# Score matmuls of two attention units, in 64-row halves of the matrix array

## The chip, the cores and the metric

The kernel runs on one core of one Trainium2 chip. A core has a matrix engine (TensorE, PE in the profile, whose weight loads are listed as PEld), a vector engine (VectorE, DVE), a scalar engine (ScalarE, ACT), a general engine (GpSimd, POOL) and a sync engine that issues DMAs (SP); they run their own instruction streams in order and wait for each other through semaphores. Matmuls read the on-chip memory SBUF (128 partitions) and write PSUM, whose banks hold 128 x 512 fp32 values each. The metric is the device time of one execution in microseconds (us).

## The reference

One transformer block over 2048 positions of width 576. The part that the change touches is an attention with 32 heads of 18 features, in 4 segments of 512 positions, with a memory carried from one segment to the next:

```python
for s in range(N):                                   # 4 segments
    qs, ks, vs = q[:, :, s], k[:, :, s], v[:, :, s]
    logits = einsum("bhqd,bhkd->bhqk", qs, ks) * scale + mask      # mask: causal, within the segment
    p = softmax(logits); a_dot = einsum("bhqk,bhkd->bhqd", p, vs)
    num = einsum("bhld,bhde->bhle", phi(qs), M); den = einsum("bhld,bhd->bhl", phi(qs), z) + 1e-6
    outs.append(g * num / den + (1 - g) * a_dot)                   # g = sigmoid(beta) per head
    M = M + einsum("bhld,bhle->bhde", phi(ks), vs); z = z + sum_l phi(ks)
x = x + ga * (concat(outs) @ wo)
x = x + gb * ((silu(h @ w_gate) * (h @ w_up)) @ w_down)            # h: normalised x, F = 4608
```

Everything is fp32. The kernel reaches that accuracy with products of split numbers: a value is a high part, rounded to the matrix engine's fp32r form, plus a low part, and a product is high*high + low*high + high*low.

## The kernel before, in words

The program has three stages, one after the other on the matrix engine.

**Projections (0 to about 234 us of the span).** For each segment the normalised input is multiplied by wq, wk and wv (`proj`, `vproj`). The results go to DRAM buffers: `kD[s]` holds, for each feature, the high part twice and the low part once, `qD[s]` high, low, high. Three rows per feature times 18 features are 54 rows, so that one matmul over 54 rows forms the three split products of a head's score at once. In this stage `early()` (L262) also runs the first pass of units 0 and 1, between the projections, in an order that a scheduler picks.

**The unit loop (about 234 to 582 us).** A unit is 4 heads of one segment; there are 32 (8 per segment). The order here is written out by hand (`tc.manual_schedule`). Each unit has two passes over its causal scores.

- Pass 1 (`p1_step`, L175, matmuls on L189) finds the row maxima: for each of four blocks of 128 queries (i = 3 to 0) and each head it makes scores against n = 128 (i + 1) keys in a PSUM bank (tag `s1`, 2 buffers, with a spare bank for early units), and DVE adds the causal mask `tri` and takes the maximum (L194, one reduction a head). POOL splits the negated maxima into a high and a low part (L199 to L202), PE transposes them (`mt_a`, L208), ACT copies them out, and `put_m` (L170) sends them by DMA as two additional rows of the unit's query stack.
- Pass 2 (`p2_step`, L609, matmuls on L624) makes the transposed scores for each of four blocks of 128 keys (j = 0 to 3) against n = 512 - 128 j queries. The two additional rows meet rows of ones on the key side, so that the maxima are subtracted in the same matmul. ACT takes exp (L627) from the PSUM bank (tag `s2`, 2 buffers) to `Pt`, and POOL clears the part above the diagonal. `av_step` (L635, matmuls on L644) then multiplies by the values: four heads go to four strips of 32 output columns.

A unit's stack (`new_stack`, L121, `load_stack`, L161; 4 sets of buffers) has 108 rows for keys, two heads of 54 rows above each other, in two column blocks, plus two rows of ones. On the query side each of the four heads has its own column block of 108 rows, of which the 54 rows of the other head of the pair are zero (cleared once by ACT, L125), so that a matmul over 108 rows gives one head's scores. With two heads side by side in the query stack, pass 2 covers two heads of n = 256 or 128 with one matmul.

The loop (L1367) walks u = 0 to 32, with pass 2 of unit u and pass 1 of unit u + 2 in the same 11 steps. At each step it takes one piece of either pass (one bank of scores and its evacuation), then the events of `PAT` (L61, four patterns by unit): V0 to V3 are the value matmuls, m and n the transposed maxima, c and d the combination with the memory part, A, B, C, D, G the memory reads of the next segment, M, X, R, S, T, Z the output projection of the segment before (`wo_m`, matmuls on L753), Q, q, P, Y the preparation of wo. Feed-forward preparations for the next stage are hung onto fixed steps.

**Feed-forward (about 582 us to the end).** The two up-projections (matmuls on L1209) and the down-projection (L1318, L1337) fill the rest.

Of the kernel before, what the change touches and what calls it, by code (L numbers as in the profile page):

```python
# [15 lines left out]
P = 128  # L16
S = 2048
D = 576
# [4 lines left out]
L = 512  # L23
# [33 lines left out]
NE = 2  # L57
WQ = (0, 3, 4, 5, 6)
E1 = 3
E2 = 2  # L60
PAT = (["", "M0", "V2 V3 m E D", "n", "M1 Q G", "c", "M2 d", "V0", "h A0 q M3 R S X", "T Y Z B0", "A1 P V1 z B1 f C"],  # L61
# [3 lines left out]
LNA = 1  # L65
S1B, S2B, XB, WB = 2, 2, 2, 1


def f32(ap):
    return ap.bitcast(F32)  # L70
# [3 lines left out]
def block(ctx: ExitStack, tc: tile.TileContext, x, wqk, wv, wo, beta, wgu, wd, c, w_mod, wm01, out):  # L74
    nc = tc.nc
# [7 lines left out]
    def chain(*g):  # L83
        for a in g:
            yield from a
# [20 lines left out]
    ident = cst.tile([P, P], F32, tag="ident", name="ident")  # L106
# [3 lines left out]
    ones = cst.tile([P, P], F32, tag="ones", name="ones")  # L110
# [5 lines left out]
    NB = 4  # L116
    sk = pool(mid, "sk")
    mwk = pool(mid, "mwk", 2)
    qst, kst = {}, {}

    def new_stack(b, stk):  # L121
        qst[b] = stk.tile([P, 4, L], F32R, tag=f"qs{b}", name=f"qs{b}")
        kst[b] = stk.tile([P, 2, L], F32R, tag=f"ks{b}", name=f"ks{b}")
        for a in range(0, 4, 2):
            nc.scalar.mul(qst[b][:, a:a + 2].rearrange("p a (b c) -> p (a b) c", c=P),  # L125
                          ones.unsqueeze(1).to_broadcast([P, 8, P]), 0.0)
        nc.sync.dma_start(f32(kst[b][108:110]).rearrange("p a (b c) -> p (a b) c", c=P),
                          ones[0:2, :].unsqueeze(1).to_broadcast([2, 8, P]))

    tri = vst.tile([P, L], F32, tag="tri", name="tri")  # L130
    nc.gpsimd.memset(tri, 0.0)
# [23 lines left out]

    units = [(s, q) for s in range(NSEG) for q in range(8)]
    NU = len(units)
    mcol, pmt, mrow = {}, {}, {}
    turn = [0, 0]

    def load_stack(u, b):  # L161
        s, q = units[u]
        for e in range(2):
            v = [d[s].rearrange("f z t -> (f z) t").rearrange("(Q a e r) t -> Q e r a t", Q=8, a=2, e=2)[q, e]
                 for d in (kD, qD)]
            r = slice(54 * e, 54 * e + 54)
            nc.sync.dma_start(f32(kst[b][r]), v[0])
            nc.sync.dma_start(f32(qst[b][r, e:4:2, :]), v[1])

    def put_m(u, b):  # L170
        mr = mrow.pop(u)
        for a in range(2):
            nc.sync.dma_start(f32(qst[b][108 + a:109 + a]).rearrange("p a t -> p (a t)"), mr[16 * a:16 * a + 16])

    def p1_step(u, b, i, ps, jp, jb, spare=0):  # L175
        if i == 3:
            mcol[u] = (mwk.tile([P, 4, 4], F32, tag="mx", name="mx"),
                       mwk.tile([P, 2, 4, 4], F32R, tag="mc", name="mc"))
        mx, mc = mcol[u]
        n = 128 * (i + 1)  # L180
        per = L // n if n <= 256 else 1
        for h0 in range(0, 4, per):
# [5 lines left out]
            for h in range(h0, h0 + per):  # L188
                nc.tensor.matmul(bank[:, n * (h - h0):n * (h - h0) + n],  # L189
                                 lhsT=qst[b][0:108, h, 128 * i:128 * i + 128],  # L190
                                 rhs=kst[b][0:108, h // 2, 0:n], start=True, stop=True)
            for h in range(h0, h0 + per):
                junk = jp.tile([P, L], BF16, tag="junk", name="junk", bufs=jb)
                nc.vector.tensor_tensor_reduce(junk[:, :n], bank[:, n * (h - h0):n * (h - h0) + n], tri[:, L - n:],  # L194
                                               1.0, -3e38, op0=ALU.add, op1=ALU.max, accum_out=mx[:, h, i:i + 1])
            if h0 + per < 4:
                yield
        if i == 0:
            nc.gpsimd.tensor_scalar(mc[:, 0], mx, -1.0, 0.0, op0=ALU.mult, op1=ALU.add)  # L199
            lo = mwk.tile([P, 4, 4], F32, tag="ml", name="ml")  # L200
            nc.gpsimd.tensor_tensor(lo, mx, f32(mc[:, 0]), op=ALU.add)
            nc.gpsimd.tensor_scalar(mc[:, 1], lo, -1.0, 0.0, op0=ALU.mult, op1=ALU.add)  # L202
        yield

    def mt_a(u, ps, tag, bufs):
        mc = mcol.pop(u)[1]
        pmt[u] = ps.tile([P, L], F32, tag=tag, name="pmt", bufs=bufs)
        nc.tensor.transpose(pmt[u][:32, :P], f32(mc).rearrange("p a b c -> p (a b c)"), ident)  # L208

    def mt_b(u):  # L210
        mrow[u] = mr = mwk.tile([32, P], F32, tag="mr", name="mr")
# [41 lines left out]
    with ExitStack() as p1:  # L253
# [5 lines left out]
        wk = pool(p1, "wk1", 2)  # L259
        ps = pool(p1, "ps1", 2, space=PSUM)  # L260

        def early():  # L262
            for u in range(2):
                load_stack(u, u)
            for u in range(NE):
                yield from p1_unit(u, u, ps, "m", 1, pb, 2)
            load_stack(2, 2)

# [65 lines left out]
        with ExitStack() as p0:  # L334
# [12 lines left out]
            for i in range(4):  # L347
                mv, rs = ln_stats(wk, [xs[0][:, i, :]], 1)
# [7 lines left out]
            for k in (4, 0, 1, 2, 3):  # L356
                for p in (1, 0):
                    for h in range(2):
                        r = 64 * (1 - p) + 32 * h
                        a = slice(0, P) if k < 4 else slice(64 - 64 * p, 128 - 64 * p)  # L360
                        w = wm[:, 1 + 2 * k + p] if k < 4 else wm[a, 0]
                        last = nc.tensor.matmul(pr[r:r + 32, :320], lhsT=sgb[a, k, :], rhs=w[:, 256 * h:256 * h + 320],
                                                start=(k == 4), stop=(k == 3))
# [10 lines left out]
            for b in range(3):  # L374
                n = P if b < 2 else 64
# [7 lines left out]
        pb = pool(p1, "pb", 2)  # L383
# [151 lines left out]
        for s in range(NSEG):  # L535
# [5 lines left out]
            g = chain(*gens)  # L541
# [6 lines left out]
            for t in QKORD:  # L548
# [4 lines left out]
                f = proj(s, t)  # L553
# [45 lines left out]
        if u < NU:  # L599
            load_stack(u, u % NB)  # L600

    def p1_seq(u):
        if NE <= u < NU:
            for i in range(4):
                yield from p1_step(u, u % NB, 3 - i, ps, wk, 4, WB if u < 11 else 0)

    Pt, av = {}, {}

    def p2_step(u, j):  # L609
        if u >= NU:  # L610
            return
        n = L - 128 * j
        per = L // n if n <= 256 else 1
        pt = pp_.tile([P, 4, n], F32, tag=f"P{j}", name="Pt", bufs=1)
        Pt[u, j] = pt
        for h in range(0, 4, per):
            turn[1] += 1
            if u < 4 and turn[1] % 3 == 0:
                bank = ps.tile([P, L], F32, tag="x", name="s2", bufs=XB)
            else:  # L620
                bank = ps.tile([P, L], F32, tag="s2", name="s2", bufs=S2B)
            for g in range(h, h + per, 2):
                w = min(per, 2)
                nc.tensor.matmul(bank[:, n * (g - h):n * (g - h + w)].rearrange("p (a b) -> p a b", a=w),  # L624
                                 lhsT=kst[u % NB][0:110, g // 2, 128 * j:128 * j + 128],
                                 rhs=qst[u % NB][0:110, g:g + w, 128 * j:L], start=True, stop=True)
            nc.scalar.activation(pt[:, h:h + per, :n], bank[:, :n * per].rearrange("p (a b) -> p a b", a=per),  # L627
                                 AF.Exp, scale=SCALE)
            if h + per < 4:
                yield  # L630
        nc.gpsimd.affine_select(out=pt[:, :, :P], in_=pt[:, :, :P], pattern=[[0, 4], [1, P]], compare_op=ALU.is_ge,
                                fill=0.0, base=0, channel_multiplier=-1)
        yield
# [725 lines left out]
    def is_plain(t, p):  # L1359
        return t == 0 or p >= NPR - 2  # L1360

    with tc.manual_schedule():
        new_stack(3, sk2)
        for j in range(4):
# [2 lines left out]
        for u in range(NU + 1):  # L1367
            s, q = divmod(u, 8)
            load_unit(u + 3)
            ga = chain(*[p2_step(u, j) for j in range(4)])  # L1370
            gb = p1_seq(u + 2)
            for k in range(11):
                next(ga, None)
                next(gb, None)
                if u == 17 and k == 0:
                    stage_a()
                if u == 24 and k == 0:
                    stage_b()
                for ev in PAT[q // 4 * 2 + u % 2][k].split():
                    event(ev, u)  # L1380
# [277 lines left out]
```

## Time and profile before

| | |
|---|---|
| median of 3 runs | 1870.63 us (1869.6 to 1871.35) |
| profiled execution, own time (first to last instruction, its span) | 1871.4 us |
| PE, share of the span | 1851.8 us, 99% |
| DVE | 1496.0 us, 80% |
| ACT | 967.5 us, 52% |
| POOL | 489.2 us, 26% |
| granted TensorE clock, mean | 0.999 |
| pass 2 score matmuls, L624 | 384, 147.5 us busy |
| pass 1 score matmuls, L189 | 512, 140.1 us busy |

A row of the profile names the line, the engine, the operation, the tiles as out<-in, the shape (for a matmul also rows*columns of the array), the count, and then the busy time in us, the mean duration in ns of one, and the engine's idle time before them with what ended it. Matmuls are pipelined: a duration spans from issue to the end of its drain, so several overlap, and what one costs is read from the interval to the next start. A table by stretches gives for each window its length, then the busy time of each engine with its number of instructions, then the granted clock and the DMA traffic. Span, busy times and intervals come from one execution.

### The profile page before, as it was taken

Reading aid. Unit: us, or ns where it says so; the run is one execution under the profiler, and the core shown is the slowest. Engines: PE = TensorE matmul, PEld = TensorE weight load, DVE = VectorE, ACT = ScalarE, POOL = GpSimd, SP = SyncE. Lnnn points to the kernel's source line nnn. Section 1 sums busy time; section 2 is a strip of 40 time slices with the busy share of each in tenths; the row PEclk is TensorE's granted clock in tenths of the full one; section 3 lists DMA queues with packets and bytes.
Section 4 is the critical chain, followed back from the end, with each engine's and each line's share of the span. In section 5 each row is a group of like instructions: output and inputs, shape, how many; then the busy total and the mean of one; then the engine's idle time right before and its main releaser. Section 6 shows DMA issues by size and latency. Waiting matters only on the chain.

```text
span 1871.4 us, 30687 instructions
## 1 busy us (share of the span) xinstructions
PE 1851.8 (99%) x10933; PEld 1562.6 (83%) x10933; DVE 1496.0 (80%) x3309; ACT 967.5 (52%) x2113; POOL 489.2 (26%) x685
## 2 busy tenths in 40 slices
PE   8999999999999999999999999999999999999999
PEld 5988866777767888888888888888888888888888
DVE  7566388888886887988888889758888888888886
ACT  7444467667676645445445444434444454444441
POOL 2010045453565244554553544300000000000000
PEclk9999999999999999999999999999999999999999
DMA  8767655447556755555455444385332333333331
GB/s 302 249 221 243 219 158 151 146 144 204 162 149 233 246 188 171 164 176 195 155 167 174 147 143 161 128 286 179 119 100 89 126 104 95 108 104 126 103 101 51
DMA packets 177585, 303.43 MB, mean 162 GB/s; under 512 B 25976, under 2 KB 107512, under 8 KB 175512
## 3 DMA queue, kind: packets, MB, share of 16 engines
q1 hardware_dynamic: 150056, 247.61, 41.9%
q10 hardware_dynamic: 27376, 53.86, 8.1%
q8 instruction: 86, 1.41, 0.3%
q14 instruction: 67, 0.55, 0.1%
HBM read 187.53 MB, written 113.33 MB: 161 GB/s over the span
## 4 chain that ended last, share of the span: by engine, by line
PE 92%; DVE 3%; DMA 3%; ACT 1%; issue 1%; SPq 0%; POOL 0%; ACTq 0%; DVEq 0%
PE A L1209 23%; PE pd L1337 13%; PE C L1209 12%; PE pd L1318 10%; PE pp L100 6%; PE B L1209 6%; PE s L624 4%; PE s L189 4%; PE av L644 4%; PE pv L100 3%; PE pw L753 3%; DMA y<-yD 1%; PE pn L810 1%; PE px L665 1%; PE pm L458 1%; DVE junk L194 1%
## 5 line engine op out<-in xcount | busy, mean ns | idle before, releaser
L1209 PE MATMUL A<-y,wh 128*128 128x512 f32 x1152 | 406.9, 394 | 3.1 <-DMA y<-yD 2.0
L194 DVE CUSTOM_DVE_ANT_0 junk<-s,tri 128x256 bf16<-128x256 f32 (+3 forms) x512 | 226.4, 486 | 57.1 <-PE s L189 50.3
L1209 PEld LDWEIGHTS A<-y,wh 128*128 128x128 f32 x1152 | 217.1, 188 | 47.8 <-ACT B L1255 2.3
L1174 DVE TENSOR_TENSOR wl<-O,wh 128x256 fp32r<-128x256 f32 x504 | 247.7, 497 | 2.2 <-ACT wh L1173 1.7
L1209 PE MATMUL A<-y,wl 128*128 128x512 f32 x576 | 227.3, 395 | 0.0
L627 ACT ACTIVATE Pt<-s 128x512 f32<-128x512 f32 (+1 forms) x352 | 186.0, 559 | 73.4 <-PE s L624 67.9
L1323 DVE TENSOR_TENSOR acc<-acc,pd 128x576 f32<-128x576 f32 x216 | 162.3, 752 | 58.8 <-PE pd L1318 51.5
L1209 PE MATMUL C<-y,wh 128*128 128x512 f32 x576 | 202.9, 393 | 0.5 <-DVE cu L1232 0.5
L1173 ACT CAST wh<-O 128x256 fp32r<-128x256 f32 x504 | 197.6, 405 | 2.1 <-issue 1.1
L1347 DVE TENSOR_TENSOR acc<-acc,pd 128x576 f32<-128x576 f32 x156 | 116.9, 750 | 93.8 <-PE pd L1337 93.3
L1337 PE MATMUL pd<-dh,ah 128*128 128x288 f32 x640 | 189.2, 296 | 0.5 <-DVE x L1341 0.5
L1337 PE MATMUL pd<-dh,al 128*128 128x288 f32 x640 | 189.1, 295 | 0.0
L1337 PE MATMUL pd<-dl,ah 128*128 128x288 f32 x640 | 188.9, 295 | 0.0
L1164 POOL TENSOR_TENSOR O<-O 128x384 f32<-128x384 f32 x132 | 149.6, 1147 | 139.6 <-DVE wl L1174 29.1
L1278 ACT CAST ah<-sg 128x512 fp32r<-128x512 f32 x192 | 119.1, 620 | 77.0 <-DVE sg L1233 70.7
L624 PE MATMUL s<-qs,ks 110*128 110x512 f32 (+2 forms) x384 | 147.5, 401 | 1.4 <-ACT nm L819 0.6
L1279 DVE TENSOR_TENSOR al<-sg,ah 128x512 fp32r<-128x512 f32 x192 | 138.8, 723 | 9.7 <-ACT ah L1278 9.5
L189 PE MATMUL s<-ks,qs 108*128 108x256 f32 (+3 forms) x512 | 140.1, 325 | 0.9 <-DMA qs<-qD 0.2
L1318 PE MATMUL pd<-dh,ah 128*128 128x288 f32 x448 | 133.0, 297 | 0.0
L1318 PE MATMUL pd<-dh,al 128*128 128x288 f32 x448 | 132.5, 296 | 0.0
L1318 PE MATMUL pd<-dl,ah 128*128 128x288 f32 x448 | 132.3, 295 | 0.0
L1337 PEld LDWEIGHTS pd<-dh,ah 128*128 128x128 f32 x640 | 120.9, 189 | 6.9 <-DVE x L1341 0.8
(370 smaller groups left out, 4335.0 us busy)
## 6 DMA issues: line engine op xcount, KB each, us to landing
O<-in_wgu_dram SPq DMA_DIRECT2D x36, 768.0 KB
O<-oD SPq DMA_DIRECT2D x36, 512.0 KB
oD<-O ACTq DMA_DIRECT2D x34, 512.0 KB
ks<-kD SPq DMA_DIRECT2D x64, 216.0 KB
qs<-qD SPq DMA_DIRECT2D x64, 216.0 KB
O<-in_wgu_dram SPq DMA_DIRECT2D x36, 384.0 KB
rD<-wr ACTq DMA_DIRECT2D x36, 336.0 KB
wr<-rD SPq DMA_DIRECT2D x35, 336.0 KB
```

What stands on the lines that cost most here:

```text
L100: nc.tensor.matmul(ps, lhsT=a, rhs=b, start=(k == 0), stop=(k == 13))
L189: nc.tensor.matmul(bank[:, n * (h - h0):n * (h - h0) + n], lhsT=qst[b][0:108, h, 128 * i:128 * i + 128], rhs=kst[b][0:108, h // 2, 0:n], s ...
L194: nc.vector.tensor_tensor_reduce(junk[:, :n], bank[:, n * (h - h0):n * (h - h0) + n], tri[:, L - n:], 1.0, -3e38, op0=ALU.add, op1=ALU.max ...
L624: nc.tensor.matmul(bank[:, n * (g - h):n * (g - h + w)].rearrange("p (a b) -> p a b", a=w), lhsT=kst[u % NB][0:110, g // 2, 128 * j:128 * ...
L627: nc.scalar.activation(pt[:, h:h + per, :n], bank[:, :n * per].rearrange("p (a b) -> p a b", a=per), AF.Exp, scale=SCALE)
L1164: eng.tensor_tensor(o[:, d], o[:, a], o[:, b], op=op)
L1173: nc.scalar.copy(wh, o)
L1174: later.append(lambda: nc.vector.tensor_tensor(wl, o, f32(wh), op=ALU.subtract))
L1209: nc.tensor.matmul(bank, lhsT=a, rhs=b, start=(first and n == 0), stop=(n == 6), skip_group_check=not first)
L1318: nc.tensor.matmul(pd[:, i, :288], lhsT=a[:, tk], rhs=w, start=(k == 0), stop=(k == 2))
L1323: nc.vector.tensor_tensor(o, o, pd[:, :, :288], op=ALU.add)
L1337: nc.tensor.matmul(pd[:, i, :288], lhsT=a[:, tk], rhs=w, start=(k == 0), stop=(k == 5))
```

## The change: what it does

The rows of a stack are laid out anew. Head e of a pair now starts at row 64 e, for keys and queries alike, with the two rows of maxima (and of ones) right behind its 54 rows. A matmul takes 54 rows (pass 1) or 56 rows (pass 2) of one half of the array, rows 0 to 63 or 64 to 127, by 128 columns. The query stack shrinks from four column blocks to two, and its zero rows and their clearing by ACT go. Pass 2's merged matmuls for two heads become one for each head, 512 in place of 384 in all; its narrowest step (n = 128) takes two banks in place of one, and so two exponentials of 256 elements for one of 512. The same split applies to pass 1 in the loop: 12 pieces a unit in either pass where there were 11, 480 matmuls as before.

A new event `a` in `PAT` makes one piece of both passes together (`scores`): a bank for each, then their matmuls in turns, pass 2 in one half and pass 1 in the other (the lists HS1 and HS2 put heads of opposite parity beside each other), then their evacuations. PAT has 12 of them per unit, for the most part in twos, and the other events are placed anew around them.

Units 0 and 1, whose first pass runs among the projections, keep full-array matmuls over 118 rows (L198 of the new file): for them one zero-padded query tile `qe`, cleared by POOL, is loaded as well, one buffer for both units, so unit 1's load stands behind unit 0's matmuls. The key stack's rows 54 to 63 and 118 to 119 are filled with ones by two DMAs in place of one.

```diff
 def new_stack(b, stk):
-    qst[b] = stk.tile([P, 4, L], F32R, ...)
+    qst[b] = stk.tile([P, 2, L], F32R, ...)
-    for a in range(0, 4, 2):
-        nc.scalar.mul(qst[b][:, a:a + 2]..., ones..., 0.0)
-    nc.sync.dma_start(f32(kst[b][108:110])..., ones[0:2, :]...)
+    for r, n in ((54, 10), (118, 2)):
+        nc.sync.dma_start(f32(kst[b][r:r + n])..., ones[0:n, :]...)
...
+HS0 = [[[0, 1, 2, 3]], [[0, 1], [2, 3]]] + [[[0], [1], [2], [3]]] * 2
+HS1 = [[[1], [0], [3], [2]], [[1, 3], [0, 2]]]
+HS2 = [[[0], [1], [2], [3]], [[0, 2], [1, 3]]]
...
 def load_stack(u, b):
-        r = slice(54 * e, 54 * e + 54)
+        r = slice(64 * e, 64 * e + 54)
         nc.sync.dma_start(f32(kst[b][r]), v[0])
-        nc.sync.dma_start(f32(qst[b][r, e:4:2, :]), v[1])
+        nc.sync.dma_start(f32(qst[b][r]), v[1])
+        if u < NE:
+            nc.sync.dma_start(f32(qe[u][r, e:4:2, :]), v[1])
...
 # pass 1, in the loop
-                nc.tensor.matmul(bank[...], lhsT=qst[b][0:108, h, 128 * i:128 * i + 128], rhs=kst[b][0:108, h // 2, 0:n], ...)
+            r = slice(64 * (h % 2), 64 * (h % 2) + 54)
+            nc.tensor.matmul(bank[...], lhsT=qst[b][r, h // 2, 128 * i:128 * i + 128], rhs=kst[b][r, h // 2, 0:n], ...)
...
 # pass 2
-            for g in range(h, h + per, 2):
-                w = min(per, 2)
-                nc.tensor.matmul(bank[...], lhsT=kst[u % NB][0:110, g // 2, 128 * j:128 * j + 128],
-                                 rhs=qst[u % NB][0:110, g:g + w, 128 * j:L], ...)
+            for o, g in enumerate(hs):
+                def mm(o=o, g=g, bank=bank):
+                    r = slice(64 * (g % 2), 64 * (g % 2) + 56)
+                    nc.tensor.matmul(bank[...], lhsT=kst[u % NB][r, g // 2, 128 * j:128 * j + 128],
+                                     rhs=qst[u % NB][r, g // 2, 128 * j:L], ...)
+                mms.append(mm)
...
+def scores(ga, gb, ma, mb):
+    next(ga, None)
+    next(gb, None)
+    while ma or mb:
+        for m in (ma, mb):
+            if m:
+                m.pop(0)()
+    next(ga, None)
+    next(gb, None)
...
-PAT = (["", "M0", "V2 V3 m E D", "n", "M1 Q G", "c", "M2 d", "V0", "h A0 q M3 R S X", "T Y Z B0", "A1 P V1 z B1 f C"],
+PAT = (("a", "a", "M0 a a", "V2 V3 m E D n", "a a", "M1 G c", "Q a a", "V0 M2 d", "a a", "h A0 q M3 R S P X T f a Y B0", "a Z A1 V1 z B1 C"),
```

(The other three patterns change in the same manner.)

More of the change, by code (lines that the diff above doesn't have):

```diff
@@ L207, in mt_a @@
         pmt[u] = ps.tile([P, L], F32, tag=tag, name="pmt", bufs=bufs)
-        nc.tensor.transpose(pmt[u][:32, :P], f32(mc).rearrange("p a b c -> p (a b c)"), ident)
+        nc.tensor.transpose(pmt[u][:32, :P], f32(mc).rearrange("p e z a c -> p (e z a c)"), ident)
     def mt_b(u):
@@ L262, in early @@
         def early():
-            for u in range(2):
+            q_ = pb.tile([P, 4, L], F32R, tag="qe", name="qe", bufs=1)
+            nc.gpsimd.memset(f32(q_), 0.0)
+            qe[0] = qe[1] = q_
+            for u in range(NE):
                 load_stack(u, u)
-            for u in range(NE):
                 yield from p1_unit(u, u, ps, "m", 1, pb, 2)
```

85 lines of the change are left out of this document (47 added, 38 removed), and 6 rows, old and new, of the table PAT.

## The prediction

> **What bounds the kernel now.** I read the page first, for the engines' shares and the score lines; then the table of stretches, to find what limits the stage that the change touches; then the engine timelines inside one unit, for intervals; last the groups by shape. From the page:
>
> ```profile
> span 1871.4 us, 30687 instructions
> ...
> PE 1851.8 (99%) x10933; PEld 1562.6 (83%) x10933; DVE 1496.0 (80%) x3309; ACT 967.5 (52%) x2113; POOL 489.2 (26%) x685
> ...
> L194 DVE CUSTOM_DVE_ANT_0 junk<-s,tri 128x256 bf16<-128x256 f32 (+3 forms) x512 | 226.4, 486 | 57.1 <-PE s L189 50.3
> ...
> L624 PE MATMUL s<-qs,ks 110*128 110x512 f32 (+2 forms) x384 | 147.5, 401 | 1.4 <-ACT nm L819 0.6
> ...
> L189 PE MATMUL s<-ks,qs 108*128 108x256 f32 (+3 forms) x512 | 140.1, 325 | 0.9 <-DMA qs<-qD 0.2
> ```
>
> The reader is to see that the matrix engine (PE) is busy nearly throughout, and that 50.3 of the 57.1 us that the vector engine (DVE) stood idle ahead of its row maxima (L194) were ended by score matmuls, while the score matmuls themselves (L624, L189) stood idle for 1.4 and 0.9 us. The reductions wait for PE, not the reverse. Now by stretches: before the unit loop, the loop while both passes run (234 to 563), its fullest part, its tail.
>
> ```profile
> core 0: us, PE busy (x) PEld busy (x) DVE busy (x) ACT busy (x) POOL busy (x), PEclk, DMA share, GB/s
> 0.00:234.00 234.00, 226.13 (x1344) 194.41 (x1345) 136.00 (x320) 116.93 (x206) 21.52 (x55) 1.00 0.71 247
> 234.00:563.00 329.00, 326.52 (x2443) 232.75 (x2441) 278.56 (x1147) 227.97 (x478) 166.76 (x344) 1.00 0.56 159
> 245.40:262.90 17.50, 17.34 (x134) 11.18 (x130) 16.11 (x72) 12.42 (x27) 7.49 (x15) 1.00 0.51 148
> 563.00:582.00 19.00, 18.30 (x137) 11.36 (x136) 8.22 (x30) 14.84 (x33) 12.88 (x22) 1.00 0.25 83
> ```
>
> Only 329 of 1871 us can change much. There PE is at 326.5/329 = 99%, DVE at 278.6/329 = 85%, ACT at 69%. So the stage is bound by PE, but DVE stands close behind: in its fullest part it reaches 16.11/17.50 = 92%. Whatever PE gains, the stage cannot go below 279 us, because the change takes no reduction off DVE.
>
> **Prices, from the PE timeline of one unit** (start, duration, then the work; the interval to the next start is the price).
>
> ```profile
> 395.65 0.34 PE L189 MATMUL s<-ks,qs 108*128 108x384 f32 x1
> 395.82 0.39 PE L624 MATMUL s<-qs,ks 110*128 110x512 f32 x1
> ...
> 397.72 0.40 PE L189 MATMUL s<-ks,qs 108*128 108x256 f32 x2
> 397.95 0.68 PE L810 MATMUL pn<-mbd,pq 128*128 128x152 f32 x4
> 398.37 0.50 PE L624 MATMUL s<-qs,ks 110*128 110x256 f32 x2
> 398.71 0.56 PE L189 MATMUL s<-ks,qs 108*128 108x128 f32 x4
> 399.20 0.85 PE L644 MATMUL av<-Pt,vq 128*32 128x384 f32 x8
> 399.98 0.50 PE L624 MATMUL s<-qs,ks 110*128 110x512 f32 x1
> 400.32 0.40 PE L189 MATMUL s<-ks,qs 108*128 108x512 f32 x1
> 400.56 0.40 PE L624 MATMUL s<-qs,ks 110*128 110x512 f32 x1
> ...
> 401.43 0.40 PE L624 MATMUL s<-qs,ks 110*128 110x512 f32 x1
> 401.66 0.40 PE L189 MATMUL s<-ks,qs 108*128 108x512 f32 x1
> 401.99 0.86 PE L644 MATMUL av<-Pt,vq 128*32 128x256 f32 x16
> 402.78 0.28 PE L208 MATMUL pmt<-ident,mc 128*32 128x128 f32 x1
> 402.82 0.48 PE L624 MATMUL s<-qs,ks 110*128 110x512 f32 x1
> 403.13 0.40 PE L189 MATMUL s<-ks,qs 108*128 108x512 f32 x1
> ```
>
> A 512-column score matmul costs 0.24 us (400.32 to 400.56), a 384 one 0.17 (395.65 to 395.82, taken as 0.175), a 256 one 0.115 (397.72 to 397.95 for two), a 128 one 0.10 (398.71 to 399.20 for four, less 0.09 for the switch priced below).
>
> **What is removed: half of the score streaming.** The first pass (p1) has four heads of each width per unit: 4 x (0.24 + 0.175 + 0.115 + 0.10) = 2.52 us. The second pass (p2) now has eight matmuls at 512 and 384, two of 512 (two heads each) and two of 256: 0.96 + 0.70 + 0.48 + 0.24 = 2.38 us. Together 4.90 us a unit. After the change each head's 54 rows lie in one half of the array, p2 of unit u issued beside p1 of unit u + 2 in the other half, head by head (p2's merged ones are split up). If halves run side by side a unit costs 2.52 us and saves 2.38; 30 units have both passes: 71.4 us. Units 30 and 31 have p2 alone and lose 0.14 each, 0.3 us.
>
> Do parts of the array run side by side here? Two groups by shape and two weight-load rows of the timeline:
>
> ```profile
> L644 PE MATMUL av<-Pt,vq 128*32 128x512 f32 x256 | 34.1, 605 | 0.0
> ...
> L362 PE MATMUL pr<-wm,sgb 64*32 64x320 f32 x8 | 1.3, 732 | 7.5 <-DMA wm<-in_wm_dram 7.5
> ```
>
> ```profile
> 386.41 0.53 PEld L189 LDWEIGHTS s<-ks,qs 108*128 108x128 f32 x4
> 387.01 0.16 PEld L644 LDWEIGHTS av<-Pt,vq 128*32 128x32 f32 x8
> ```
>
> The av matmuls, in four column strips, sum to 256 x 0.605 = 155 us of durations in 34.1 us of busy time: they overlap. The eight of 64 rows do likewise (5.9 us in 1.3), though in column strips too; no row shows 64 x 128 halves alone. Eight strip loads take 0.16 us together; four whole loads take 0.53, with 0.19 for one (386.41 row less three intervals of 0.11). I take overlap of both loads and streams, the nearest rows, and keep the other ends as rivals.
>
> **What is added on PE: changes of shape.** The price from the rows: into the strips, 401.66 to 401.99 is 0.33 instead of 0.23 (+0.10). Out of them, eight av of 384 take 0.78 (399.20 to 399.98) against four streams of 0.175 = 0.70 (+0.08), and the first full matmul after takes 0.34 or 0.31 instead of 0.24 (399.98, 402.82; +0.07 to 0.10, its weights come late). A round trip is 0.27 us. The Trainium skill, "TensorEngine Tiling (Array Packing)", section "Tiling Modes", says that changing the mode, and not merely the tile, drains TensorE; the trace agrees with +0.10 for column strips, and no run here shows it yet for row halves. In the instruction order of the built programs, from the first to the last score matmul, changes between full array, strips and halves rise from 194 to 387: 96.5 more round trips, 26 us. Bounds: 0.17 each (no late weights: 16 us) to 0.45 (both halves wait for a whole 0.19 load: 43 us). The nearest row is 0.27.
>
> PE's need falls to 326.5 - 71.1 + 26 = 281 us of the 329.
>
> **What then ends the stage: DVE.** DVE needs 278.6 us. It is filled to 92% where it has most to do and to 85% on average with PE as the limit. I take 91%: 278.6/0.91 = 306 us, with PE then at 281/306 = 92%, two engines feeding each other through two banks a pass. Ends: 97% (287 us) and no gain. The stage saves 23 us (ends 42 and 0).
>
> **The rest.** p2's narrowest step becomes two exponentials of 256 elements instead of one of 512:
>
> ```profile
> L627 ACT ACTIVATE Pt<-s 128x512 f32<-128x512 f32 x223 | 127.0, 599 | 49.7 <-PE s L624 45.2 <-POOL mc L199 2.0 <-POOL Pt L631 0.8
> L627 ACT ACTIVATE Pt<-s 128x384 f32<-128x384 f32 x128 | 60.0, 489 | 23.7 <-PE s L624 22.7
> ```
>
> 110 ns per 128 elements leaves 159 ns fixed, so 0.16 x 32 = 5 us more on ACT, hidden in its 101 idle us of the stage; uncovered it would be 5 us. The ScalarE zeroings of the stacks go, worth nothing, since PE is covered there. In front, units 0 and 1 keep a zero-padded copy (qe), one buffer for both. Unit 1's load must wait on SP for unit 0's last score matmuls, and behind it queue the kD and qD stores and the w_mod loads. In the built order 16 projection matmuls of 512 columns (0.24 each) and 8 transposes (0.1 each) stand between that and unit 1's first score matmul, 4.6 us; a load landing later stalls PE: 0 to 1.5 us, I take 0.5. The qe clear on POOL is hidden (21.5 of 234 us busy). The tail from 563 (+0.3) and everything after 582 stay.
>
> Sum: 1871.4 - 23 + 0.5 + 0.3 = 1849.2 against the profiled span; the median of the runs, 1870.63, is 0.8 below that span. I say 1849.
>
> **Rivals.**
> 1. The halves do not run side by side. PE then pays 2.52 + 2.52 in place of 4.90 (+0.14 x 32 = 4.5 us) and the switches, 16 to 43, most likely 26: slower, 1892 to 1919, at 1902. For: no row shows a lone row half. Against: L644 and L362 overlap. It decides once the overlap takes back less than those 30 us.
> 2. Streams overlap but the two weight loads queue, 0.11 each. A pair then costs 0.24, 0.22, 0.22, 0.22: 3.60 us a unit, saving 1.30 x 30 = 39 us; less 26 leaves 13: 1858 (at 0.45 a switch 1875). For: the 0.53 us of four loads. Against: the 0.16 us of eight. The Trainium skill, "TensorE: Matmul & The Clock Gate", section "LDWEIGHTS", holds that a load's time goes by columns and not by rows, so a half load would be no shorter; the 0.19 us of L189 is 128 columns, and no half load is in this trace.
> 3. PE waits for banks. A joint step needs a bank from DVE and one from ACT, and PE waits for the later in order. The 45 us that PE saves over 12 x 30 steps is 0.125 us a step: a mean wait of that size eats everything (1871), 0.18 makes it 1890. For: weight loads of s wait for the exponentials already (row below). Against: those waits are mostly covered by the matmul before.
>
> ```profile
> PEld s L624 <- ACT Pt L627: 28.7, 46, 0.9
> ```
>
> **Numbers.** Forecast (1830 to 1866) 0.55; rival 1 0.20; rival 2 0.15; rival 3 0.10. A difference of 0.2%, 3.7 us, is about what a measurement of this kernel can tell from none. Faster: 0.55 + 0.11 of rival 2 = 0.66. Same: 0.03 from rival 2 and 0.04 from rival 3 = 0.07. Slower: the rest, 0.27. Range: 1830 (DVE at 97%) up to 1892, the cheap end of rival 1; left out are rival 1's dearer part (0.12) and a gain beyond 42 us or a little more (0.07).
>
> **What would show it.** In the profile after, score rows at 54 and 56 rows, with count times mean well above busy time, and about 2.5 us of PE starts a unit for both passes: the halves overlap. The start after a run of score matmuls late by about 0.1, and first ones late by another: the price of switches. DVE in the loop near 91%, its waits for score matmuls below 50.3 us, PE's own waits for banks up: DVE has become the limit. PE still at 99% and DVE at or under 85%: rival 1 or 2, told apart by whether starts come in twos. The prediction is wrong if the halves queue, if a switch costs 0.4 us or more, or if both engines wait for each other.

## The result, and the profile after

The changed kernel takes 1885.19 us (median of four runs, 1878.65 to 1886.96) against 1870.12 before: 1.0072 of it, interval 1.0059 to 1.0085. It is slower by 0.72%, where a gain to 1849 us was predicted. Its runs spread with the granted clock: 1878.65 at a mean clock of 0.998 (the profiled one), 1883.75 to 1886.96 at 0.992 to 0.994; the kernel before has 0.999 to 1.0.

The page of the changed kernel, the lines that answer to those of before (pass 2's score matmuls are now on L639, pass 1's on L187, the maxima on L206):

```profile
span 1876.9 us, 30994 instructions
...
PE 1846.5 (98%) x11061; PEld 1519.5 (81%) x11061; DVE 1493.8 (80%) x3309; ACT 961.4 (51%) x2137; POOL 490.9 (26%) x686
...
L206 DVE CUSTOM_DVE_ANT_0 junk<-s,tri 128x256 bf16<-128x256 f32 (+3 forms) x512 | 224.7, 486 | 61.8 <-PE s L187 52.5
...
L639 PE MATMUL s<-qs,ks 56*128 56x256 f32 (+3 forms) x512 | 141.0, 365 | 6.2 <-ACT Pt L645 5.5
L187 PE MATMUL s<-ks,qs 54*128 54x512 f32 (+1 forms) x480 | 138.9, 374 | 3.8 <-DMA qs<-qD 1.8
```

The table of stretches: the projections, the part of the loop with both passes, 7 us at the loop's beginning, and the loop's end.

```profile
core 0: us, PE busy (x) PEld busy (x) DVE busy (x) ACT busy (x) POOL busy (x), PEclk, DMA share, GB/s
0.00:237.00 237.00, 226.78 (x1346) 193.73 (x1347) 137.25 (x320) 109.87 (x198) 23.66 (x56) 1.00 0.72 247
237.00:567.00 330.00, 319.96 (x2556) 191.30 (x2556) 278.02 (x1148) 228.87 (x507) 166.94 (x343) 0.99 0.57 159
250.00:257.00 7.00, 7.00 (x45) 3.82 (x49) 5.40 (x24) 4.62 (x11) 2.15 (x4) 0.51 0.47 141
567.00:587.50 20.50, 19.91 (x148) 11.40 (x149) 8.10 (x29) 15.70 (x36) 12.53 (x22) 1.00 0.25 81
```

The reader is to see three things. The projections end 3 us later (237 for 234). The stage that was to shrink to 306 us takes 330: PE is still busy for 97% of it, DVE for 84%. And at the loop's beginning PE ran for 7 us at half clock though it was busy throughout.

One row measures the steady part without the two ends: the 30 transposed maxima of units 2 to 31 (first and last start). First the kernel before, then the changed one:

```profile
L208 PE MATMUL pmt<-ident,mc x30: 283/284/286, 245.4 to 567.1; 128*32 128x128 f32 x30
```

```profile
L221 PE MATMUL pmt<-ident,mc x30: 283/284/396, 251.3 to 571.6; 128*32 128x128 f32 x30
```

321.7 us before, 320.3 after. So 29 units gained 1.4 us, not some 22; 5.9 us were lost ahead of unit 2's row; behind the last row come 1304.3 and 1305.3 us. Each row is one execution, and 5.5 us of the changed one lie at half clock (250.0 to 256.8), which is worth about 2.7 us by an estimate: the gain is a few us at the most.

**The halves do run side by side.** The PE timeline of the changed kernel inside one unit (start, duration, work):

```profile
388.29 0.38 PE L639 MATMUL s<-qs,ks 56*128 56x256 f32 x1
388.30 0.38 PE L187 MATMUL s<-ks,qs 54*128 54x256 f32 x1
388.52 0.28 PE L639 MATMUL s<-qs,ks 56*128 56x256 f32 x1
388.52 0.39 PE L187 MATMUL s<-ks,qs 54*128 54x256 f32 x2
388.64 0.28 PE L639 MATMUL s<-qs,ks 56*128 56x256 f32 x1
388.75 0.28 PE L187 MATMUL s<-ks,qs 54*128 54x256 f32 x1
388.76 0.28 PE L639 MATMUL s<-qs,ks 56*128 56x256 f32 x1
388.96 0.40 PE L771 MATMUL pw<-wol,oh 128*128 128x288 f32 x1
389.20 0.30 PE L771 MATMUL pw<-woh,ol 128*128 128x288 f32 x1
389.33 0.30 PE L771 MATMUL pw<-woh,oh 128*128 128x288 f32 x1
...
392.26 0.85 PE L662 MATMUL av<-Pt,vq 128*32 128x384 f32 x8
393.05 0.50 PE L639 MATMUL s<-qs,ks 56*128 56x512 f32 x1
393.05 0.72 PE L187 MATMUL s<-ks,qs 54*128 54x512 f32 x2
393.39 0.39 PE L639 MATMUL s<-qs,ks 56*128 56x512 f32 x1
393.70 0.40 PE L771 MATMUL pw<-woh,oh 128*128 128x288 f32 x1
393.94 0.29 PE L771 MATMUL pw<-wol,oh 128*128 128x288 f32 x1
```

Pairs start together and a pair of 256 costs what one cost before (388.52, 388.64, 388.75). Of 480 possible pairs in the loop 394 start within 10 ns of each other. The weight loads do the same:

```profile
393.05 0.18 PEld L639 LDWEIGHTS s<-qs,ks 56*128 56x128 f32 x1 [0.62 <-ACT nm L837]
393.05 0.29 PEld L187 LDWEIGHTS s<-ks,qs 54*128 54x128 f32 x2
```

**What a run of halves costs in switches** is in the same rows. Eight av of 384 columns take 0.79 us (392.26 to 393.05) where four streams of 0.175 make 0.70: +0.09. The first pair takes 0.34 instead of 0.24, its successor 0.31, because the array changes back behind it: +0.10 and +0.08. The first full matmul takes 0.24 (393.70 to 393.94) where the later pw take 0.13: +0.11. Together 0.38 us for one run of halves. That is one place, and its first weight load is listed as waiting for ACT; the run at 388.29, whose first load is not, has +0.11 on its first pair as well (388.29 to 388.52 is 0.23 instead of 0.115). The chain is visible in the waits of the weight loads too (total us, times, longest), the loop of the kernel before first:

```profile
PEld s L624 <- ACT Pt L627: 31.8, 53, 0.9
PEld av L644 <- issue: 9.2, 34, 0.4
PEld s L624 <- issue: 0.8, 1, 0.8
PEld pw L753 <- issue: 0.8, 2, 0.6
```

```profile
PEld s L639 <- ACT Pt L645: 33.5, 87, 1.0
PEld pw L771 <- issue: 17.0, 59, 0.8
PEld s L639 <- issue: 16.9, 84, 0.8
PEld av L662 <- issue: 14.1, 58, 0.7
PEld s L187 <- DVE mx L206: 8.9, 28, 0.7
```

"Issue" is idle time behind which the profile shows no other engine. On the loads of pw, pass 2 and av it comes to 48.0 us in 201 places, against 10.8 in 37.

### The profile page after: what moved, and what is told of

It reads as the page before. It is cut to its first block, busy times and chain, and to the rows that moved or that the text cites. A ratio compares the mean times of both kernels' runs of the same rounds, so it can differ in the third digit from the quotient of the medians.

```text
span 1876.9 us, 30994 instructions
## 1 busy us (share of the span) xinstructions
PE 1846.5 (98%) x11061; PEld 1519.5 (81%) x11061; DVE 1493.8 (80%) x3309; ACT 961.4 (51%) x2137; POOL 490.9 (26%) x686
## 4 chain that ended last, share of the span: by engine, by line
PE 89%; DVE 4%; DMA 4%; ACT 2%; issue 1%; POOL 1%; SPq 0%; ACTq 0%; DVEq 0%
PE A L1227 23%; PE pd L1355 13%; PE C L1227 12%; PE pd L1336 10%; PE B L1227 6%; PE pp L100 5%; PE s L639 5%; PE av L662 4%; PE pw L771 3%; PE pv L100 3%; PE s L187 2%; DMA y<-yD 1%; PE pn L828 1%; PE px L683 1%; ACT Pt L645 1%
## 5 line engine op out<-in xcount | busy, mean ns | idle before, releaser
L206 DVE CUSTOM_DVE_ANT_0 junk<-s,tri 128x256 bf16<-128x256 f32 (+3 forms) x512 | 224.7, 486 | 61.8 <-PE s L187 52.5
L1192 DVE TENSOR_TENSOR wl<-O,wh 128x256 fp32r<-128x256 f32 x504 | 245.3, 492 | 2.1 <-ACT wh L1191 1.6
L645 ACT ACTIVATE Pt<-s 128x512 f32<-128x512 f32 (+2 forms) x384 | 183.1, 525 | 79.9 <-PE s L187 61.3
L1296 ACT CAST ah<-sg 128x512 fp32r<-128x512 f32 x192 | 119.2, 621 | 77.6 <-DVE sg L1251 71.4
L639 PE MATMUL s<-qs,ks 56*128 56x256 f32 (+3 forms) x512 | 141.0, 365 | 6.2 <-ACT Pt L645 5.5
L187 PE MATMUL s<-ks,qs 54*128 54x512 f32 (+1 forms) x480 | 138.9, 374 | 3.8 <-DMA qs<-qD 1.8
L1297 DVE TENSOR_TENSOR al<-sg,ah 128x512 fp32r<-128x512 f32 x192 | 133.6, 696 | 10.7 <-ACT ah L1296 10.5
L649 POOL TENSOR_SCALAR_AFFINE_SELECT Pt<-Pt 128x512 f32<-128x512 f32 x128 | 81.5, 637 | 183.5 <-ACT Pt L645 182.9
```

The lines of the kernel that those rows point to most:

```text
L187: nc.tensor.matmul(bank[:, n * o:n * o + n], lhsT=qst[b][r, h // 2, 128 * i:128 * i + 128], rhs=kst[b][r, h // 2, 0:n], start=True, stop=True)
L206: nc.vector.tensor_tensor_reduce(junk[:, :n], bank[:, n * o:n * o + n], tri[:, L - n:], 1.0, -3e38, op0=ALU.add, op1=ALU.max, accum_out=mx ...
L639: nc.tensor.matmul(bank[:, n * o:n * o + n], lhsT=kst[u % NB][r, g // 2, 128 * j:128 * j + 128], rhs=qst[u % NB][r, g // 2, 128 * j:L], st ...
L645: nc.scalar.activation(pt[:, hs[0]:hs[-1] + 1:2, :n], bank[:, :n * per].rearrange("p (a b) -> p a b", a=per), AF.Exp, scale=SCALE)
L1192: later.append(lambda: nc.vector.tensor_tensor(wl, o, f32(wh), op=ALU.subtract))
```

## The experiments

The experiments ask: is the overlap real and what is it worth (same order with full rows, or with both passes in the same half); what do shape changes cost with the waits for banks nearly gone (light evacuations, together and one engine alone); where does the loss at the loop's beginning come from (loads, order, front, clock).

**All rows, the changed order.** The changed kernel with the old stacks (zero-padded, 108 and 110 rows) and a joint step's matmuls still in turns.

```diff
-            r = slice(64 * (h % 2), 64 * (h % 2) + 54)
-            nc.tensor.matmul(..., lhsT=qst[b][r, h // 2, ...], rhs=kst[b][r, h // 2, 0:n], ...)
+            nc.tensor.matmul(..., lhsT=qst[b][0:108, h, ...], rhs=kst[b][0:108, h // 2, 0:n], ...)
...
```

> The order of the changed kernel (its PAT, its joint score steps, one matmul a head), but on the old stacks: 108 and 110 rows of the full array with zero rows, so nothing runs side by side and the mode changes of the row halves go. Theory 1 (streams do overlap and save some 69 us of PE time in the loop; dearer mode changes take back 46 and waits for banks 23): the full-array version has the 69 us and lacks the 46, so it stands near the changed kernel, 1875 to 1895. Theory 2 (the new order itself is what costs, the halves give nothing): it is as slow as the changed kernel or slower, above 1895. Theory 3 (DVE is the limit whatever PE does): 1878 to 1885, with DVE as full as in the changed kernel.

Measured 1878.2 us, 1.0039 of before (1.0024 to 1.0054), at full clock from 12.8 us to the end. It is faster than the changed kernel. Its steady row:

```profile
L219 PE MATMUL pmt<-ident,mc x30: 272/284/286, 246.0 to 575.1; 128*32 128x128 f32 x30
```

329.1 us: against that order the halves gain 8.8 us in the steady part. But the order itself, with pass 2's merged matmuls split, costs 7.4 us against the 321.7 of before. What the halves gain is gone elsewhere: the changed kernel's steady row begins 5.3 us later (251.3 for 246.0), 3.3 us more stand behind it, and in most of its runs the clock is lower. Theories 1 and 3 both hold this time in their ranges, so the run excludes only theory 2.

**Both passes in the same half.**

```diff
-HS1 = [[[1], [0], [3], [2]], [[1, 3], [0, 2]]]
+HS1 = [[[0], [1], [2], [3]], [[0, 2], [1, 3]]]
```

> The changed kernel with one list altered, so that the two matmuls of a pair use the same 64-row half: everything else, mode changes too, is equal, only the overlap is gone. Theory 1: PE needs 69 us more in the loop, part of which fills its waits for banks (23 us): 1925 to 1955. If the loop is bound by DVE or ACT: under 1900. If the halves never overlapped: no change, 1885.

Measured 1895.86 us, 1.0135 (1.012 to 1.0151): 10.7 us over the changed kernel, and far below the 1925 that theory 1 expected. The time lies where 'bound by DVE or ACT' put it, but the run cannot decide, because it takes away a part of the overlap and not all: in two joint steps in a row the second matmul of one still meets the first of the next, and between 290 and 560 us 104 pairs of score matmuls start within 10 ns of each other, against 310 in the changed kernel. What it showed beside the price is the clock:

```profile
237.50:241.00 3.50, 3.03 (x16) 1.53 (x14) 1.94 (x7) 2.90 (x7) 0.26 (x1) 1.00 0.53 211
241.00:261.50 20.50, 20.34 (x102) 10.53 (x104) 12.48 (x54) 9.31 (x21) 6.63 (x12) 0.50 0.54 140
```

PE was busy for 20.34 of 20.50 us and had half the clock all that time.

**Light evacuation, changed kernel and kernel before.**

```diff
-  nc.vector.tensor_tensor_reduce(junk[:, :n], bank[:, n * o:n * o + n], tri[:, L - n:], ...)
+  nc.vector.tensor_tensor_reduce(junk[:, :64], bank[:, n * o:n * o + 64], tri[:, L - n:L - n + 64], ...)
-  nc.scalar.activation(pt[:, ..., :n], bank[...], AF.Exp, ...)
+  nc.scalar.activation(pt[:, ..., :64], bank[...][:, :, :64], AF.Exp, ...)
...
```

> The changed kernel with lighter evacuations: each row maximum over the first 64 keys of its block only, each exponential over the first 64 columns only (the rest of Pt stays at one), so attention is left incomplete; PE's work is unchanged. What is left is PE's own need, streams and mode changes. Theory 1: the 23 us and more of bank waits and the half-clock stretches go: 1840 to 1862. Theory 2 (mode changes alone took everything): hardly moves, above 1870. Theory 3 (evacuation is the limit): below 1840.

> The kernel before with the same lighter evacuations (maxima and exponentials over 64 columns, the rest left out). PE bounds it, so all theories expect little: 1860 to 1870. The difference to the lighter changed kernel is what the change is worth to PE alone: theory 1 says 10 to 25 us in favour of the changed kernel.

Measured 1855.74 us, 0.9915 (0.9898 to 0.9931), for the changed kernel and 1862.92, 0.9957 (0.9943 to 0.9972), for the kernel before. So light evacuation is worth 29.5 us to the changed kernel and 7.2 to the old one: waiting for banks costs the change some 22 us by the medians. A part of that is clock: at 0.998 the changed kernel takes 1878.65 and at 0.997 its light version 1855.8, 22.9 us less, which leaves some 16. The steady rows, the changed kernel's first:

```profile
L221 PE MATMUL pmt<-ident,mc x30: 283/284/396, 250.5 to 551.0; 128*32 128x128 f32 x30
```

```profile
L208 PE MATMUL pmt<-ident,mc x30: 283/284/285, 246.8 to 558.8; 128*32 128x128 f32 x30
```

300.5 against 312.0 us. With the evacuation made light the change gains 11.5 us in 29 units, 0.40 a unit. The prediction's PE terms say 71.4 - 26 = 45 us in 30 units, 1.5 a unit. Most of the expected gain is therefore missing on PE itself. The stage of both, the changed kernel's first:

```profile
core 0: us, PE busy (x) PEld busy (x) DVE busy (x) ACT busy (x) POOL busy (x), PEclk, DMA share, GB/s
237.00:547.00 310.00, 302.10 (x2555) 181.35 (x2554) 165.88 (x1150) 138.67 (x508) 170.81 (x347) 0.98 0.61 169
```

```profile
235.60:555.40 319.80, 318.20 (x2437) 233.10 (x2435) 166.20 (x1151) 138.07 (x480) 170.99 (x347) 1.00 0.57 164
```

PE is busy for 302.1 us of it instead of 318.2. Of the 302.1 about 5 are owed to a half-clock stretch (10.2 us from 246.7 on), so PE itself gains some 21 us where 45 were forecast.

To see where, I set each start of PE from the first score matmul to the last of pass 1 against its steady interval (0.235 us at 512 columns and so on, a pair counted once). In the light runs the steady intervals sum to 297.7 us before and 236.2 after, a saving of 61.5; the excess over them is 21.9 us before and 73.9 after. The old order has 182 changes of shape, the new one 357: charged with the whole excess, a round trip costs 0.24 us before and 0.41 after. That is an upper bound: the 73.9 also hold the 5 us of half clock and 7.9 us in which PE stood idle (310.0 less 302.1), the 21.9 only 1.6 of the latter. Without these the excess rises from some 20 to some 61 us, by 41.

**Light exponentials alone, light maxima alone.**

> The changed kernel, but the exponentials of pass 2 take 64 columns a head instead of all (the rest of Pt stays 1.0, so the attention's weights are left out in part); DVE's maxima are whole. The light-evacuation run took 29.5 us off the changed kernel with both engines lightened. Theory 'ACT sets the wait' (the changed kernel's score loads waited 33.5 us on the exponentials and 8.9 on the maxima): most of it comes back here, 1860 to 1867. Rival 'DVE sets it' (it is 84 to 92 per cent filled): at most a third, 1875 to 1883. Third: a joint step needs both banks, so that one alone gives little, and the two single gains sum to clearly less than 29.5.

> The changed kernel, but DVE takes each row maximum over the first 64 keys only (the maxima are left out in part); the exponentials are whole. Theory 'ACT sets the wait': 1878 to 1883. Rival 'DVE sets it': 1860 to 1870. Third, both banks are needed: this and the run with light exponentials sum to clearly less than 29.5 us.

Measured 1878.63 us (1.0043, 1.0026 to 1.006) with light exponentials and 1866.61 (0.999, 0.9978 to 1.0001) with light maxima: 6.6 and 18.6 us below the changed kernel, 25.1 together, against 29.5 for both at once. That is what the rival expected: DVE is the engine waited for more, although the waits listed above name ACT first (33.5 against 8.9 us): PE takes its banks in order, and the list shows the one that came last. The pairs say the same. Of 480 possible ones, 394 start within 10 ns in the changed kernel, 393 with light exponentials, 450 with light maxima and 448 with both: it is DVE's banks that tear pairs apart. The sizes are less sure, because the clock of these runs varied (0.992 to 0.998). At 0.998 light maxima take 1865.7 to 1866.6 us in five runs, 12 to 13 below the changed kernel's 1878.65; at 0.992 light exponentials take 1880.1, 6.5 below its 1886.63. Both together then stand against some 23, so that a few us need both engines at once.

**Three attempts at the loop's beginning and at the order.** Stack 3 loaded among the projections, so that no query load is waited for at the loop's start; the maxima's transposes and value matmuls set between the widest joint steps; both.

```diff
...
-                for b in range(3):
+                for b in range(4):
                     new_stack(b, sk)
...
-        new_stack(3, sk2)
...
-PAT = (("a", "a", "M0 a a", "V2 V3 m E D n", "a a", "M1 G c", "Q a a", "V0 M2 d", "a a", ...
+PAT = (("a", "a", "V2 V3 m a a", "M0 E D n", "M1 a a", "G c", "Q a a", "V0 M2 d", "a a", ...
```

> The changed kernel with the stack of unit 3 allocated and loaded during the projections, as those of units 0 to 2 are, in place of at the start of the loop (two small work tiles of the projection stage get one buffer instead of two to make room). The changed kernel's trace shows PE standing still for 1.8 us at 246 us for this load, and the granted clock at one half from 250 to 257. Theory (the idle time at the loop's start, with half-height matmuls, drops the clock, and that is also what spreads the changed kernel's runs from 1878.65 to 1886.96): no half-clock stretch in the loop, runs within 2 us of each other, 1868 to 1877. Rival (half-height matmuls drop the clock by themselves, without idle time): half-clock stretches stay, 1880 or more.

> The changed kernel with V2, V3 and m placed between the two groups of 512-column score steps, where M0 stood, and M0 behind them (in the second pattern V1 also goes behind the last group). In the trace the second 512 group is where PE waits for banks, 0.45 us a unit in units 9 to 20 and up to 0.5 to 0.7 in the first eight, against the version with light evacuations. Theory (waits for banks come from groups that follow each other too closely): 5 to 12 us less than the changed kernel, 1873 to 1880. Rival (the evacuating engines are simply full): no change, the wait appears at another group, 1883 to 1888.

> Both edits. If both theories hold they add up: 1860 to 1870, level with or below the kernel before. If the clock stretch is only moved, 1872 or more.

Measured 1886.06 us (1.0083, 1.0065 to 1.0102), 1886.85 (1.0086, 1.0069 to 1.0103) and 1890.93 (1.0106, 1.0089 to 1.0122): none gains. With the stack loaded early the wait for a query load is gone from the trace, yet half clock is granted for 17.1 us from 245.6 on: the drop does not come from that wait. The loop starts 4 us later; why is not settled, since unit 0's transposed maxima already come 5.6 us later (103.2 for 97.6), ahead of any load of that stack, and the run also takes a buffer each from two work tiles. The other order left PE's idle time for banks of scores as it was (6.4 us in the loop against 6.6) and did not shorten it (321.4 us in the steady row against 320.3).

**Halves in the loop, the old front.** The query stack keeps four zero-padded blocks, and units 0 and 1 use it; no tile `qe`.

```diff
...
-            q_ = pb.tile([P, 4, L], F32R, tag="qe", name="qe", bufs=1)
-            nc.gpsimd.memset(f32(q_), 0.0)
-            qe[0] = qe[1] = q_
-            for u in range(NE):
-                load_stack(u, u)
+            for u in range(2):
+                load_stack(u, u)
+            for u in range(NE):
```

> All of the change but its new front: the query stack keeps four zero-padded column blocks (cleared by ACT as before), units 0 and 1 use it for their first pass, and no second query tile with one buffer is loaded; every score matmul in the loop is in row halves. Theory: the 1.5 us stall at unit 1's transposed maxima and the later loop start go (first score matmul at about 235 instead of 237.8), worth 2 to 3 us, and the half-clock stretch behind the loop's start stays, since the halves make it: 1881 to 1884. Rival 'the clock drops because PE idled in front and at the loop's start': the stretch goes too, 1874 to 1878.

Measured 1874.68 us, 1.0028 (1.0013 to 1.0042): 10.5 us below the changed kernel. The time is the rival's, the trace is the theory's. The stall in front is gone; in the changed kernel it is this row:

```profile
PE pmt L221 <- POOL mc L215: 1.5, 1, 1.5
```

But the half clock is not gone. Its windows, the last 3.4 us at full clock and the 17 behind:

```profile
235.00:238.40 3.40, 3.26 (x14) 1.80 (x13) 2.27 (x7) 3.03 (x7) 0.38 (x1) 1.00 0.61 234
238.40:255.40 17.00, 17.00 (x90) 8.36 (x92) 11.61 (x54) 9.18 (x20) 6.51 (x12) 0.50 0.64 165
```

PE had been busy for 3.26 of 3.40 us, so the theory that its idle time in front brings the drop falls. The front (first score matmul at 235.0 instead of 237.8) and the 1.8 us of waiting for the query load at the loop's start explain 4.6 of the 10.5 us; in most of its runs the clock was 0.995 or 0.996, and 0.992 to 0.994 in three of four of the changed kernel, which fits the rest. Both fills still go through SP here. Their wait is missing because PE, at half clock from 238.4 on, comes to the query load only at 245.4; in the next run, at full clock, it waits for it until 245.3.

**Full rows in the first 8, and in the first 3 units.** As the run before, with all rows in the joint steps of the first units. In the second kernel POOL issues the second fill of ones for stack 3, so that SP has as many DMAs as before ahead of that stack's loads.

```diff
-            r = slice(64 * (h % 2), 64 * (h % 2) + 54)
+            r = slice(0, 118) if u - 2 < TH else slice(64 * (h % 2), 64 * (h % 2) + 54)      # TH = 8, 3
...
-            nc.sync.dma_start(f32(kst[b][r:r + n])..., ones[0:n, :]...)
+            (nc.gpsimd if b == 3 and r > 64 else nc.sync).dma_start(...)                     # TH = 3 only
```

> As the run without the second query tile, but the joint steps of the loop's first 8 units use all rows of the array (zero-padded), and row halves come from unit 8 on. Theory 'row halves lower the granted clock where they are densest, at the loop's beginning': no half-clock stretch before 590, 2 to 3 us of overlap lost in 8 units, 1874 to 1878. Rival 'row halves lower the clock wherever they begin': a stretch of half clock of 7 us or more behind unit 8 (about 320), 1880 to 1886.

> As the run with full rows in 8 units, but with full rows in the loop's first 3 units only, and stack 3's second fill of ones issued by POOL instead of SP (before, one fill went through SP; two put stack 3's loads behind a store and PE idled 1.6 to 1.8 us for them). If the change in its steady part is worth nothing and the loss lies in the front, the loop's start and the half clock there, the run comes out level with the kernel before: 1869 to 1873, first score matmul at about 235, no wait on a query load at 244 to 247, no half clock before 280. Rival 'the clock drops wherever halves begin': a stretch of half clock behind unit 3 (about 270) and 1875 to 1880.

Measured 1878.15 us (1.0042, 1.0027 to 1.0057) with 8 units and 1871.97 (1.0011, 1.0002 to 1.002) with 3. In neither trace is there a half clock at the loop's beginning. With 8 units two stretches of 3.4 us come late, at 534 and 558, none behind unit 8 as the rival had it; PE waits 1.6 us for stack 3's query load at the loop's start. With 3 units there is no such wait, and no stretch comes in the loop of the profiled execution, the fastest of eleven; three others, at 0.997, took 1875 to 1876 us, and where their clock fell is not known. The same windows of the run with 3 units:

```profile
235.00:238.40 3.40, 3.29 (x13) 2.20 (x14) 2.75 (x9) 3.03 (x8) 0.64 (x1) 1.00 0.79 300
238.40:255.40 17.00, 16.86 (x132) 11.13 (x133) 15.02 (x68) 11.79 (x27) 8.07 (x16) 1.00 0.62 162
```

and its steady row:

```profile
L223 PE MATMUL pmt<-ident,mc x30: 283/284/287, 245.9 to 565.2; 128*32 128x128 f32 x30
```

This closes the sum by medians: 1885.2 for the change; 10.5 less without the new front; 2.7 less with full rows in the first three units and the fill moved to POOL; the 1.5 us that are left stand at the edge of what can be told from the kernel before. The steady part takes 319.3 us against 321.7, one execution each. No run beat the kernel before with the whole computation in it.

## Why the prediction was wrong

**Overlap of the halves: right.** Starts come in twos, a few ns apart, streams and weight loads alike. Rivals 1 and 2 fall. Not all of the gain arrives: where one pass's bank is late a pair is torn apart (394 pairs of 480, 448 with light evacuation), and the steady intervals fall by 61.5 us even in the light runs, not 71.4.

**The step that failed: the changes of shape, and with them PE's need of 281 us.** I took 0.27 us a round trip from the column strips and charged it for the 96.5 that are added: 26 us. The trace has 0.38 around one run of halves, which for 96.5 is 37 us, and the accounting of the light runs gives 41 for the 87.5 up to the last of pass 1 (52 if all of its excess is charged). A run of halves pays four late starts, and I had counted three: beside the strips only the full matmuls got their weights late, beside the halves both sides do (+0.10 and +0.11). Out of the strips the price stayed what it was (+0.09 and +0.10 into halves, +0.08 and +0.07 to 0.10 into full rows). My own upper bound, 0.45 (43 us), would have been nearer. So PE's need fell by some 21 us and not by 45, to between 297 us (the light run, 302.1 less 5) and 305 (326.5 - 21) instead of 281. That leaves little of the 306 us at which I let the stage end for any wait; and the stage of the light runs, from the first score matmul to the last of pass 1, fell from 319.7 to 310.2 us. The prediction's last sentence names a switch of 0.4 us as what would make it wrong; the measured one is about that. The Trainium skill, "TensorEngine Tiling (Array Packing)", section "Tiling Modes", says that a change of mode drains the engine. The trace agrees for row halves (+0.09 on entry), but that is under half of the price: 0.17 on entry and exit, 0.21 for the first weights that come late on either side.

**DVE as the next limit: half right.** I expected it at 91% and the stage at 306 us. It stands at 84%, PE at 97%, and DVE's idle time that score matmuls ended rose to 52.5 us instead of falling below 50.3. By the prediction's own reading that would have meant rival 1 or 2, told apart by paired starts; it had no place for "the pairs are there and the switches eat them". Yet light maxima alone bring 18.6 us by the medians and 12 to 13 at the same clock: DVE is waited for, bank by bank, long before it is full.

**Rival 3, waits for banks, had a chance of 0.10 and is the second cause.** It costs the change 22 us more than the kernel before by the medians, some 16 at the same clock, 10 in the steady rows (19.8 against 9.7 us from light evacuation). The Trainium skill, "TensorEngine Tiling (Array Packing)", section "PSUM Bottleneck", warns that tiling speeds up the matmuls and not the evacuation of PSUM. These runs agree. Neither cause alone ends at 1885.

**The front: wrong in size.** 0.5 us was forecast, 1.5 at most. The first score matmul of the loop starts 2.8 us late (237.8 for 235.0): unit 1's pass is pushed back by the one-buffer query tile, but what stalls is PE's transpose of unit 1's maxima, 1.5 us on POOL, not the score matmuls behind the load. And I costed the two fills of ones at nothing: with the additional DMA on SP one more of stack 3's loads is issued behind a store, and PE waits 1.8 us for the query load after it (the score line of the page, above). Between the runs with 8 and with 3 units of full rows, both at full clock there, the 1.6 us of this wait go when POOL issues the fill.

**The clock: not foreseen.** Of the 36 us between forecast and result 21 lie in the steady part and 4 in front and at the loop's start; some 11 are left for the clock and what it drags along. That split is worked out, not measured part by part; 6.5 of the 11 are the distance between the median and the profiled execution.

**The range** held the time by luck: it reached so far because of the place it left for rival 1, and the time came there for another reason.

## What to carry to other kernels

Price a change of array shape on both sides, the switch and the late first weights, and from rows of the shapes that are switched between; here 0.4 us a round trip between full rows and halves, so a run of two pairs, which saves 0.23 us of streaming at 256 columns and 0.47 at 512, hardly pays for itself. When two streams are joined in one step, every step needs both consumers' banks at once, so a consumer at 84% is already a limit; a run with light evacuation of both kernels separates the two. When buffers are rearranged, count each new DMA on its queue: one small fill more cost 1.8 us here, more than the 1.4 us of the steady part.

## What the runs showed of the hardware

Row halves in the loop's first units bring the granted clock down while PE is busy. Each of the nine profiled executions with halves there has a half-clock stretch in that place, 6.8 to 20.5 us long, in steps of about 3.4; the kernel before, its light version, the one with full rows throughout and the two with full rows in the first units have none. The Trainium skill, "TensorE: Matmul & The Clock Gate", Part 1, ties the clock to how busy PE was in a window of about 3.4 us. The lengths agree with such a window, but not the cause in that wording, since PE was busy for 96% of the 3.4 us ahead of one drop and 99% of a stretch of 20.5. Why it drops was not settled: with halves from unit 8 on, no stretch comes before 534 us. Idle time may be another way to it: in the two runs that load stack 3 early a stretch of 3.4 us also stands at 160 us, among full-row projections, and there PE had been busy for only 2.28 of 4.20 us ahead of it in one and 2.37 of 3.80 in the other.
